# Ordering the readers of a DMA transpose later, and a batch's front earlier, in a planned attention and mixer kernel

## The chip, the cores and the metric

The kernel runs on one core of a Trainium2 chip. Its metric is the device time of one execution in microseconds. It was 430.25 us in the median of six runs before the change (424.12 to 431.26). The core has five engines that each work through their own instructions in order: TensorE (PE) multiplies matrices into eight PSUM banks, VectorE (DVE) and ScalarE (ACT) do elementwise work and read those banks, GpSimd (POOL) and SyncE (SP) here mostly issue DMAs. Engines wait for one another, and for DMAs, by semaphores. A wait at the head of an engine's queue holds all that stands behind it.

## The reference

Eight batches go through attention with a low-rank projection and then through a mixer. With B = 8, H = 8 heads, S = 1024, D = 64, 64 projected keys, and H*D = 512 columns:

```python
k_proj = einsum('ks,bhsd->bhkd', E, k)
v_proj = einsum('ks,bhsd->bhkd', F, v)
scores = q @ k_proj^T / sqrt(64)
x = softmax(scores) @ v_proj                     # to (batch, 1024, 512)
h = (relu(x^T @ w_tok1) @ w_tok2)^T              # mixes tokens: 1024 -> 256 -> 1024
u = x + h
out = u + relu(u @ w_ch1) @ w_ch2                # mixes channels: 512 -> 1536 -> 512
```

Inputs and output are float32; the kernel multiplies in bfloat16.

## The kernel before, in words

**Two halves of a batch's work.** The *front* of a batch is all up to u: the projection of k and v (`kv_proj`, L467 and L470), scores and exponential (`scores`, L580 and L589), attention's product with v and its division into x_sb (`attend`, L603, L615, L620), the first token product (`token1`, or from batch 2 on `token1_seven`, L761, in seven products for eight), and the second token product with the addition of x that writes u (`token2`, L654 and L665). What follows is the channel mixer, in two blocks of 512 rows for a batch, so 16 blocks j. For each block there are four sums of quarters of turned u (`s_sums`, L694, on VectorE), six sets of up-products (`up_set`, L937), and the down-products (`down_block`, L1038), again with seven products in place of eight: three up-products of a set read turned u itself, four read the sums S. Results are added to u into one of three tiles o and stored (L1067).

**Turned u.** The up-products need u with channels on partitions. From batch 1 on, `token2` lets SP issue a DMA transpose (L674) after each four of its eight row blocks: the first half of a batch goes to uT0, the second to uT1. Each of these tiles exists once, so a transpose also has to wait until the last product of the batch before has read its half. The returned job is kept in `turned_u[b, i]`. From batch 2 on, q and the projected k are turned by DMA transposes on SP's queue too (L545 into qT, L499 from kb into kT).

**Loads take turns with transposes.** `tie` adds a dependency. k and v of batch b are loaded in four pieces by GpSimd; the first three go behind the first transpose of batch b-2 (`load_kv`), the second transpose of batch b-2 goes behind the third piece, the fourth piece behind that transpose, and the two q loads behind it as well (`q_transpose`). GpSimd's queue, L329 and L1067, holds these loads and the stores of o in one order.

**The planner.** All work is first given to a `Planner` as jobs: an engine, a time that it occupies the engine (`occ`), a time until its result is there (`lat`), what it reads and writes, and a due time (`prio`). `plan()` then walks through a model of the five engines, and at each step starts the job that can start first, among nearly equal ones the most urgent. Sorted by planned start, the jobs are emitted; `pin()` fixes the resulting order on each engine. The model's times are nowhere in the built program: only its order is, and on the chip each instruction starts when its engine and its semaphores let it. In the model a u transpose occupies the DMA for 3.5 us and ends after 5.5 us (`sp` adds 2.0), and a job on another engine that depends on it starts 1.0 us after that at the earliest. A transpose has no due time of its own; it takes one from the jobs behind it.

**Due times of a front.** `front(b, begin, end)` lists the units of a front with a cost each and spreads their due times evenly from begin to end. The main loop adds the channel mixer of batch b, and then the front of batch b+1 with begin = at - 62 and end = at - 14, where `at = 2 * TU * (b + 1)` is the model's time for the batch and TU is 24.65. So front and mixer of neighbouring batches interleave on TensorE. The front of a batch also adds `load_kv` for the batch after it.

Of the kernel before, what the change touches and what calls it, by code (L numbers as in the profile page):

```python
# [183 lines left out]
def kernel(  # L184
# [59 lines left out]
    def bank(b):  # L244

        return banks[b.at]
# [59 lines left out]
    def pe(n, cols, fn, **kw):  # L306
        t = n * MM[cols]
        return pl.add("PE", t, t, fn, **kw)

    def dve(cols, fn, ps=True, **kw):  # L310
        t = cols / 960 + 0.07 if ps else cols / 1920 + 0.07
        return pl.add("DVE", t, t + 0.09, fn, **kw)
# [5 lines left out]
    def sp(t, fn, **kw):  # L318
        return pl.add("DMA", t, t + 2.0, fn, **kw)
# [88 lines left out]
    for n, (src, dst) in enumerate(((EF[1], FT_sb), (EF[0], ET_sb))):  # L408
        b = Bank("S", full=False)
# [44 lines left out]
    def kv_proj(b, h0, hn, due, block=False):  # L454
        hs = slice(h0, h0 + hn)
        hk = slice(h0 % (H // 2), h0 % (H // 2) + hn)
        heads = range(h0, h0 + hn)
        bk = Bank(stream[0], full=False)

        def view():  # L460
            return bank(bk).rearrange("p (h d) -> p h d", d=D)

        def mm(lo, hi):
            t = view()
            for si in range(lo, hi):
                a, z = si == 0, si == NSI - 1
                nc.tensor.matmul(  # L467
                    t[0:KP, 0:hn], ET_sb[:, si, :], k_sb[:, hs, si, :], start=a, stop=z
                )
                nc.tensor.matmul(  # L470
                    t[KP : 2 * KP, 0:hn], FT_sb[:, si, :], v_sb[:, hs, si, :], start=a, stop=z
                )

        cols = hn * D
        reads = ["ET", "FT"] + [(n, h) for n in "kv" for h in heads]
        pl.add(
            "PE", 8 * max(cols, 128) / 2400 + 0.22, 8 * max(cols, 128) / 2400 + 0.22,
            lambda: mm(0, NSI), reads=reads, takes=[bk], prio=due,
            after=[("vb", i, h) for i in range(2) for h in heads],
        )  # L480
        src = [lambda: view()[0:KP, 0:hn], lambda: view()[KP : 2 * KP, 0:hn]]
        if block:
            k_to = [kb[i * KP : (i + 1) * KP, hs, i, :] for i in range(2)]
        else:
            k_to = [kp[:, hk, i, :] for i in range(2)]
        v_to = [vb[i * KP : (i + 1) * KP, hs, i, 0:D] for i in range(2)]

        def copy(to, n):
            return lambda: nc.scalar.copy(out=to, in_=src[n]())

        for i in range(2):
            act(cols, copy(k_to[i], 0), writes=[("kb" if block else "kp", i, h if block else h % (H // 2)) for h in heads], uses=[bk])
        for i in (1, 0):
            act(cols, copy(v_to[i], 1), writes=[("vb", i, h) for h in heads], uses=[bk])

    def k_transpose_dma():
        sp(
            2.5,
            lambda: nc.sync.dma_start_transpose(  # L499
                out=kT.rearrange("p h c k -> p h (c k)"), in_=kb.rearrange("p h r d -> p (h r d)")  # L500
            ),
            reads=[("kb", i, h) for i in range(2) for h in range(H)],
            writes=[("kT", i, h) for i in range(2) for h in range(H)], prio=None,
        )

    def k_transpose(h0, hn, due):
        hs = slice(h0, h0 + hn)
        heads = range(h0, h0 + hn)
        bk = Bank(stream[0], full=False)

        def view():
            return bank(bk).rearrange("p (h k) -> p h k", k=KP)

        def mm():
            for h in range(hn):
                nc.tensor.matmul(
                    view()[:, h, :], kp[:, h0 % (H // 2) + h].rearrange("k r d -> k (r d)"),
                    ident[:KP, :KP], start=True, stop=True,
                )

        pe(
            hn, 64, mm, reads=[("kp", i, h % (H // 2)) for i in range(2) for h in heads], takes=[bk],
            prio=due,
            after=[("kT", i, h) for i in range(2) for h in heads],
        )
        act(
            hn * KP, lambda: nc.scalar.copy(out=kT[0:D, hs, 0, :], in_=view()[0:D, 0:hn]),
            writes=[("kT", 0, h) for h in heads], uses=[bk],
        )
        act(  # L530
            hn * KP,
            lambda: nc.scalar.copy(out=kT[D : 2 * D, hs, 1, :], in_=view()[D : 2 * D, 0:hn]),
            writes=[("kT", 1, h) for h in heads], uses=[bk],
        )
# [114 lines left out]
    def token2(b, si, due):  # L649
        bk = Bank(stream[0], full=False)  # L650

        def mm():
            for t in range(TC):
                nc.tensor.matmul(  # L654
                    bank(bk), wt2_sb[:, t, si::NSI], hT_sb[:, t, :],
                    start=(t == 0), stop=(t == TC - 1),
                )

        pe(
            TC, 512, mm, reads=["wt2"] + [("hT", t, hp) for t in range(TC) for hp in range(HP)],  # L660
            takes=[bk], prio=due,
        )
        dve(
            512,
            lambda: nc.vector.tensor_add(  # L665
                out=u_t[b % 2][:, si, :], in0=bank(bk), in1=x_sb[:, si, :]
            ),
            reads=[("x", h, si // NJ) for h in range(H)], writes=[("u", b % 2, si)], uses=[bk],
        )
        if si % NJ == NJ - 1:  # L670
            i = si // NJ
            j = sp(
                3.5,
                lambda: nc.sync.dma_start_transpose(  # L674
                    out=uT_t[i].rearrange("p s dc q -> p (s dc) q"),
                    in_=u_t[b % 2][:, i * NJ : (i + 1) * NJ].rearrange("p s d -> p (s d)"),
                ),
                reads=[("u", b % 2, n) for n in range(i * NJ, (i + 1) * NJ)],
                writes=[("uT", i, n) for n in range(HP)], prio=None,
            )  # L680
            turned_u[b, i] = j

    def quarter(j, sh, dh):
# [481 lines left out]
    def load_kv(b):  # L1165
        first, second = turned_u.get((b - 2, 0)), turned_u.get((b - 2, 1))
        jobs = load_group(b, "kv", first)
        if second:
            tie(second, jobs[2])
            tie(jobs[3], second)  # L1170
            rest[b] = jobs[3:]

    def front(b, begin, end):
        units = []

        def unit(cost, f):
            units.append((cost, f))

        hn = H // 2 if b == 1 else H
        for i in range(H // hn):  # L1180
            if b == 1:
                unit(1.9 * hn / H, lambda t, i=i: kv_proj(b, i * hn, hn, t))
                unit(0.9 * hn / H, lambda t, i=i: k_transpose(i * hn, hn, t))
            else:
                unit(1.9, lambda t: kv_proj(b, 0, H, t - EARLY, True))
                unit(0.0, lambda t: k_transpose_dma())
            if b == 1:
                for hp in range(2 * i, 2 * i + 2):
                    unit(0.4, lambda t, hp=hp: q_transpose_pe(hp, t))
        if b + 1 < B:  # L1190
            unit(0.0, lambda t: load_kv(b + 1))
        unit(0.4, lambda t: scores(0, t))
        unit(0.4, lambda t: scores(1, t))
        for h in range(H):
            if h + 2 < H:
                unit(0.4, lambda t, h=h: scores(h + 2, t))
            for half in range(2):
                unit(0.25, lambda t, h=h, half=half: attend(h, half, t))
        if b < 2:
            for n in range(TC):  # L1200
                unit(1.8, lambda t, n=n: token1(n, t))
        else:
            unit(3.2, lambda t: token1_seven(b, t))
        for si in range(NSI):
            unit(0.55, lambda t, si=si: token2(b, si, t))
        total = sum(c for c, _ in units)
        done = 0.0
        for c, f in units:
            f(begin + (end - begin) * done / total)
            done += c  # L1210
# [4 lines left out]
    for b in range(B):  # L1215
        for j in (2 * b, 2 * b + 1):
            s_sums(j)
            for m in range(SETS):
                up_set(j, m)
            down_block(j)  # L1220
        if b == 1:
            tok1_sums()
        if b + 1 < B:
            at = 2 * TU * (b + 1)
            if b > 0:
                q_transpose(b + 1)
            front(b + 1, at - 62, at - 14)
    gate = mybir.DependencyInfo(mybir.DependencyClass.Sync, mybir.DependencyReason.DATA)
    plan = pl.plan()
    name_of = {}  # L1230
# [51 lines left out]
```

## Time and profile before

The profiled execution took 431.77 us; its span, first to last instruction, is 429.8 us.

| what | value |
| --- | --- |
| median of six runs (range) | 430.25 us (424.12 to 431.26) |
| profiled execution: time, span | 431.77 us, 429.8 us |
| mean granted TensorE clock | 0.989 |
| busy: PE, DVE, ACT, POOL | 415.4, 342.2, 228.9, 66.3 us |
| up-products (L937), four groups | 58.2, 57.6, 55.9 and 28.8 us |
| down-products (L1038), two groups | 104.1 and 78.4 us |
| u transposes, issue to landing (min, median, max) | 4.2, 5.0, 10.9 us (14 of them) |
| stores of o, issue to landing, median | 3.8 us |
| loads of k, v, q from batch 1 on, median | 7.5, 9.6, 9.9 us |

Busy times are shares of the span in which an engine has an instruction running. In the table of groups a row has the source line, engine, operation, operands and shapes, the count, the busy time, the mean length of one, and the idle time of the engine before such instructions with its releaser. The list of waits gives for each pair of waiter and releaser the time in total, how often, and the longest. A wait for several things is put down to the one that came last. PEclk is the granted TensorE clock as a share of full speed.

### The profile page before, as it was taken

Reading aid. Unit: us, or ns where it says so; the run is one execution under the profiler, and the core shown is the slowest. Engines: PE = TensorE matmul, PEld = TensorE weight load, DVE = VectorE, ACT = ScalarE, POOL = GpSimd, SP = SyncE. Lnnn points to the kernel's source line nnn. Section 1 sums busy time; section 2 is a strip of 40 time slices with the busy share of each in tenths; the row PEclk is TensorE's granted clock in tenths of the full one; section 3 lists DMA queues with packets and bytes.
Section 4 is the critical chain, followed back from the end, with each engine's and each line's share of the span. In section 5 each row is a group of like instructions: output and inputs, shape, how many; then the busy total and the mean of one; then the engine's idle time right before and its main releaser. Section 6 shows DMA issues by size and latency. Waiting matters only on the chain.

```text
span 429.8 us, 9371 instructions
## 1 busy us (share of the span) xinstructions
PE 415.4 (97%) x3755; PEld 345.0 (80%) x3778; DVE 342.2 (80%) x837; ACT 228.9 (53%) x434; POOL 66.3 (15%) x104
## 2 busy tenths in 40 slices
PE   9899999999999999969999999999999999999995
PEld 4587886788788878858878897888878898888884
DVE  2469978789798987957878996889868998968674
ACT  2858885266546454634455645375555644354430
POOL 8443221022021212110111200212100000000000
PEclk9999999999999999997999999999999999999998
DMA  9999999977999895979739895699850502250222
GB/s 164 207 200 206 206 207 177 229 119 186 186 153 229 141 221 104 198 87 147 195 76 196 170 143 156 91 217 165 170 121 6 143 1 103 46 148 15 84 99 99
DMA packets 96651, 62.47 MB, mean 145 GB/s; under 512 B 62048, under 2 KB 92256, under 8 KB 96608
## 3 DMA queue, kind: packets, MB, share of 16 engines
q0 software_dynamic: 34944, 45.09, 52.7%
q1 hardware_dynamic: 61584, 16.52, 22.5%
q8 instruction: 29, 0.48, 0.4%
q10 hardware_dynamic: 80, 0.26, 0.2%
q14 instruction: 14, 0.11, 0.1%
HBM read 59.24 MB, written 16.78 MB: 177 GB/s over the span
## 4 chain that ended last, share of the span: by engine, by line
PE 83%; DMA 7%; DVE 7%; issue 1%; ACT 1%; POOL 1%; POOLq 0%; DVEq 0%
PE ps L1038 33%; PE ps L937 31%; PE ps L654 5%; PE ps L761 3%; PE ps L603 3%; DMA q_sb<-in_q_dram 3%; PE ps L467 3%; DMA uT<-u 3%; PE ps L580 2%; DMA v_sb<-in_v_dram 2%; DVE x_sb L620 1%; DVE u L864 1%; PE ps L634 1%; DVE S L694 1%; DVE G L972 1%
## 5 line engine op out<-in xcount | busy, mean ns | idle before, releaser
L1038 PEld LDWEIGHTS <-G 128*128 128x128 bf16 x1344 | 130.4, 98 | 20.4 <-issue 0.7
L1038 PE MATMUL ps<-wc_sb,G 128*128 128x256 bf16 x768 | 104.1, 274 | 0.2
L959 ACT ACTIVATE G<-ps 128x512 bf16<-128x512 f32 x96 | 57.1, 597 | 67.6 <-PE ps L937 66.7
L937 PEld LDWEIGHTS <-wc_sb 128*128 128x128 bf16 x768 | 74.3, 98 | 12.9 <-issue 0.3
L1038 PE MATMUL ps<-wT,G 128*128 128x256 bf16 x576 | 78.4, 274 | 0.1
L937 PEld LDWEIGHTS <-wT 128*128 128x128 bf16 x576 | 55.7, 98 | 10.5 <-issue 1.3
L937 PE MATMUL ps<-uT,wc_sb 128*128 128x256 bf16 x384 | 58.2, 274 | 0.2
L937 PE MATMUL ps<-S,wc_sb 128*128 128x256 bf16 x384 | 57.6, 273 | 0.1
L937 PE MATMUL ps<-S,wT 128*128 128x256 bf16 x384 | 55.9, 276 | 0.5 <-DVE S L694 0.4
L620 DVE TENSOR_TENSOR x_sb<-ps,rdn 128x256 bf16<-128x256 f32 x128 | 49.9, 415 | 0.8
L1067 POOL DMA_DIRECT2D out_dram<-o x30 | 16.3, 545 | 211.1 <-DVE o L1073 145.4
L589 ACT ACTIVATE a<-ps 128x512 bf16<-128x512 f32 x64 | 37.7, 600 | 19.2 <-PE ps L580 16.5
L665 DVE TENSOR_TENSOR u<-ps,x_sb 128x512 bf16<-128x512 f32 x56 | 37.3, 686 | 11.6 <-PE ps L654 6.8
L965 ACT COPY ua<-ps 128x512 f32<-128x512 f32 x48 | 28.2, 587 | 29.9 <-PE ps L937 29.5
L918 DVE CUSTOM_DVE_ANT_0 G<-ps,ua 128x512 bf16<-128x512 f32 x48 | 32.8, 684 | 10.3 <-ACT ua L965 10.2
L918 DVE CUSTOM_DVE_ANT_0 g<-ps,ub 128x512 bf16<-128x512 f32 x48 | 32.8, 685 | 10.2 <-PE ps L937 10.0
L972 DVE TENSOR_TENSOR G<-G 128x512 bf16<-128x512 bf16 x96 | 38.8, 418 | 1.7
L615 DVE RECIPROCAL rdn<-ps 128x4 f32<-128x4 f32 x128 | 21.2, 177 | 21.4 <-PE ps L603 19.1
L603 PE MATMUL ps<-vb,a 128*128 128x130 bf16 x256 | 31.5, 222 | 3.9 <-DVE x_sb L620 3.9
L965 ACT COPY ub<-ps 128x512 f32<-128x512 f32 x48 | 28.0, 584 | 12.8 <-PE ps L937 12.2
L978 ACT COPY ps<-ps 128x512 f32<-128x512 f32 x48 | 27.9, 581 | 8.3 <-PE ps L937 2.8
L654 PE MATMUL ps<-hT_sb,wt_sb 128*128 128x512 bf16 x99 | 29.1, 379 | 0.5 <-issue 0.2
(90 smaller groups left out, 524.5 us busy)
## 6 DMA issues: line engine op xcount, KB each, us to landing
out_dram<-o POOLq DMA_DIRECT2D x30, 512.0 KB, 3.8
k_sb<-in_k_dram POOLq DMA_DIRECT2D x14, 512.0 KB, 7.5
v_sb<-in_v_dram POOLq DMA_DIRECT2D x14, 512.0 KB, 9.6
q_sb<-in_q_dram POOLq DMA_DIRECT2D x14, 512.0 KB, 9.9
wc_sb<-in_moe_w_ch_dram POOLq DMA_DIRECT2D x6, 256.0 KB, 12.1
wc_sb<-in_moe_w_ch_dram POOLq DMA_DIRECT2D x4, 384.0 KB, 12.4
k_sb<-in_k_dram POOLq DMA_DIRECT2D x4, 256.0 KB, 7.3
v_sb<-in_v_dram POOLq DMA_DIRECT2D x4, 256.0 KB, 7.8
```

The lines of the kernel that those rows point to most:

```text
L589: lambda: nc.scalar.activation(out=a_t[h % 4], in_=bank(bk), func=ACT.Exp, scale=scale),
L603: nc.tensor.matmul(view()[:, 2 * jj : 2 * jj + 2].rearrange("p c d -> p (c d)"), a_t[h % 4][:, j * P : (j + 1) * P], vb[:, h].rearrange("k ...
L620: lambda: nc.vector.tensor_tensor(out=x_sb[:, 4 * half : 4 * half + 4, h * D : (h + 1) * D], in0=view()[:, :, 0:D], in1=rdn[:, :, None].to ...
L654: nc.tensor.matmul(bank(bk), wt2_sb[:, t, si::NSI], hT_sb[:, t, :], start=(t == 0), stop=(t == TC - 1),)
L665: lambda: nc.vector.tensor_add(out=u_t[b % 2][:, si, :], in0=bank(bk), in1=x_sb[:, si, :]),
L918: nc.vector._custom_dve(TENSOR_ADD_SAT, out=out, in0=in0, in1=in1, s0=FMAX, s1=0.0)
L937: nc.tensor.matmul(t[:, c, :], w1_of(n, dd, 2 * m + c), a_of(j, n, dd), start=(n in (1, 7) and c == 0 and dd == 0), stop=(c == 1 and dd == 1),
L959: lambda: nc.scalar.activation(out=G[:, n, cs], in_=view(src), func=ACT.Relu),
L965: 512, lambda: nc.scalar.copy(out=dst, in_=view("y")), writes=[(name, s % 2)],
L972: 512, lambda: f(out=G[:, n, cs], in0=in0, in1=in1), ps=False, reads=deps,
L978: 512, lambda: nc.scalar.copy(out=view("y"), in_=view("x")), takes=[bk["y"]],
L1038: nc.tensor.matmul(view(where[n])[:, t, :], G[:, G_OF[n], cc, t * P : (t + 1) * P], w2_of(n, cc), start=(n in opens and t == 0 and cc == 0 ...
```

## The change

Two places change. After a u transpose of batch 2 or later has been added, its `lat` is raised by 3.0, so that the model has its result after 8.5 us in place of 5.5. And the front of batch b+1, from batch 3 on (b > 1), gets due times that are 4 us earlier at both ends.

```diff
@@ token2
                 writes=[("uT", i, n) for n in range(HP)], prio=None,
             )
+
+            if b > 1:
+                j.lat += 3.0
             turned_u[b, i] = j
@@ main loop
             at = 2 * TU * (b + 1)
             if b > 0:
                 q_transpose(b + 1)
-            front(b + 1, at - 62, at - 14)
+            ahead = 4 if b > 1 else 0
+            front(b + 1, at - 62 - ahead, at - 14 - ahead)
```

The built program has the same instructions on every engine, in another order on TensorE, VectorE, ScalarE and SP; GpSimd's order is the same.

## The prediction

> **What bounds the kernel now.** I read the page's busy table and its 40 slices first: which engine is full, and where is it not?
>
> ```profile
> span 429.8 us, 9371 instructions
> ...
> PE 415.4 (97%) x3755; PEld 345.0 (80%) x3778; DVE 342.2 (80%) x837; ACT 228.9 (53%) x434; POOL 66.3 (15%) x104
> ...
> PE   9899999999999999969999999999999999999995
> ...
> PEclk9999999999999999997999999999999999999998
> ```
>
> TensorE bounds it. Apart from start and end there is one hole, the 18th slice with a 6, and the next slice has the only lowered clock. So nothing short of removing matmuls can shorten the rest, and this change removes none. The list of waits names the hole:
>
> ```profile
> POOL v_sb L329 <- DMA uT<-u: 32.9, 5, 10.5
> ...
> DVE S L694 <- DMA uT<-u: 4.5, 2, 4.1
> ...
> PE ps L603 <- DVE x_sb L620: 3.9, 1, 3.9
> ```
>
> TensorE waited once, 3.9 us, for an x_sb multiplication; VectorE stood 4.1 us on a transpose of u at a sum S (L694). The timeline there (start, length, what, in brackets the idle time before it and its releaser) and then the chain (start, length) show that these are one event:
>
> ```profile
> 180.35 3.78 SPq L674 DMA_TRANSPOSE uT<-u  x1
> ...
> 180.79 0.55 POOL L1067 DMA_DIRECT2D out_dram<-o  x1 [1.51 <-DVE o L1103]
> ...
> 191.30 0.43 DVE L694 TENSOR_TENSOR S<-uT 128x512 bf16<-128x512 bf16 x1 [4.12 <-DMA uT<-u]
> 191.64 0.42 DVE L620 TENSOR_TENSOR x_sb<-ps,rdn 128x256 bf16<-128x256 f32 x1
> 191.84 0.75 POOL L329 DMA_DIRECT2D v_sb<-in_v_dram  x1 [10.50 <-DMA uT<-u]
> ...
> 192.11 0.59 PE L603 MATMUL ps<-vb,a 128*128 128x130 bf16 x4 [3.92 <-DVE x_sb L620]
> ```
>
> ```profile
> 180.35 10.92 DMA uT<-u
> 191.28 0.02 issue
> 191.30 0.43 DVE S L694
> 191.72 0.34 DVE x_sb L620
> ```
>
> The second transpose of batch 3 (counted from 0) needs 10.92 us to land. A store of o issued 0.44 us after it lands after 10.0 us; the median store takes 3.8, the median transpose 5.0. The two slow each other. No matmul wants that S yet; but VectorE's queue is in order, the sum stands ahead of an x_sb multiplication, and attention's next product (L603) needs the PSUM bank that this frees. The bill closes: 10.92 + 0.02 + 0.43 + 0.34 + 0.04 to the next matmul = 11.75 us after the issue; the matmuls between the issue and that L603 fill 7.85 us (58 of 256 columns at 109 ns, 4 of 512 at 216, 12 of 130 at 55, paces from the chain: six in 0.66, four in 0.86, two in 0.11). 11.75 - 7.85 = 3.90, measured 3.92.
>
> The stall costs more than itself. Busy time by stage:
>
> ```profile
> core 0: us, PE busy (x) PEld busy (x) DVE busy (x) ACT busy (x) POOL busy (x), PEclk, DMA share, GB/s
> 182.70:193.40 10.70, 6.78 (x61) 5.56 (x59) 5.60 (x19) 3.89 (x8) 1.55 (x3) 0.90 0.71 87
> 193.40:204.20 10.80, 10.80 (x84) 8.72 (x83) 8.20 (x25) 4.54 (x8) 0.70 (x1) 0.78 0.92 147
> ```
>
> Lost clock is 0.10 x 10.7 + 0.22 x 10.8 = 3.45 us of TensorE work. Cut finer, PEclk is 1.00 from 188 to 191.3 us and 0.51 from there to 198.2: it falls at the end of the stall.
>
> **The change, part by part.** No instruction is added or removed on any engine; the planner's costs and due times alone change, so everything is a matter of order. I read the order in which the built program's instructions stand, before and after. Through batch 1's transposes nothing moves.
>
> *3 us more latency of the transpose.* The S sums fall back in VectorE's queue. For the stalled half, 23 VectorE instructions stood between the last add that the transpose reads and its first sum; now 46 do, the rest of attention among them. The transpose itself still cannot start before the last product that reads the old uT1. From that product to the first matmul that depends on the sum, through VectorE's queue or directly, I count the matmuls by shape and price them as above. Stalled half (batch 3): 132 + 3 + 24 = 14.39 + 0.65 + 1.32 = 16.4 us, where 7.85 were. Second halves of batches 2, 4, 5, 6, 7: 20.9, 14.7, 17.4, 12.8, 12.2 us (before 16.7, 8.5, 9.1, 9.1, 10.9). First halves of 2 to 7, counted from the token product behind which they start: 14.7, 15.1, 14.5, 14.5, 13.0, 13.3 (before 14.2, 11.6, 9.6, 10.7, 10.7, 9.6). What is needed is a landing plus about 0.8 us. Landings in the trace are 5.4, 10.9, 4.3, 5.5, 4.8, 6.4 for the second halves and 4.2 to 6.5 for the first, which also need about 1.2 us from product to issue. Even a collision as bad as the worst in every half (11.75) fits under the smallest cover, 12.2. So the stall goes: -3.92 us, and the clock stays up.
>
> What the clock gives back is where a rule and the row part. The row says 3.45 us. The Trainium skill, "TensorE: Matmul & The Clock Gate", section "Part 1: The HAM clock gate", has the array at half rate until about 3.4 us of sustained work, an estimate of 3.4 / 2 = 1.7 us per cooling. By the rule the sum is 3.92 + 1.7 = 5.6 us, by the row 3.92 + 3.45 = 7.37. I take the row, since it is of this very stall. The page's threshold, about 3.4 us of idle time, agrees with it: this stall just reached it. It speaks against expecting the whole gain in every execution: a shorter stall may have cost no clock.
>
> *Fronts 4 us ahead.* Attention of a front ends 2.6 to 4.8 us of matmuls earlier against the products around it, the first token product starts 3 to 5.5 us earlier, and the projection of k and v for the front after it comes earlier too. That last one is the dangerous side: it needs the second half of v, which the GpSimd queue holds behind the second transpose (10.50 in the timeline), with the q loads behind it. Cover from that transpose's possible issue to the next projection was 26.4, 25.5, 25.0, 25.8 us behind batches 2 to 5; it is 22.7, 20.5, 20.5, 21.8. Needed in the worst case seen: 10.92 + 0.57 to the issue + 5.36 landing of v = 16.9. It lies beside other work, 3.6 us to spare, cost nothing; without that cover it would cost its excess and the clock. GpSimd's own order is unchanged, so its stores are not passed by anything.
>
> SP's queue does change, around the u transposes of batches 3 and 4. Batch 4's kb transpose goes ahead of q's, and the second half of its q behind the first u transpose; batch 5's kb stands between the halves of q. kT needs 6.7 us from the projection's last matmul (159.39) to landing (166.06) and has 15.7 us or more. The late half of q has about 19 us after the token product; a u and a q transpose in a row took 8.1 us (117.95 to 126.03). Batch 5's kb waits for q to land: at worst 10.92 + 12.2 (191.28 to 203.47) = 23.1 us after the u transpose's issue, while kb itself is ready after 20.5 + 3.3 = 23.8. Cost nothing.
>
> *Bank and engine hand-overs.* Attention meets other up-products than before, and the trace of before cannot show the new meetings. Bounds: below zero is excluded on TensorE, since its gaps after 60 us other than the stall sum to under 0.6 us; above, the nearest rows are single waits of 0.4 us (PE on S, on kT), and a dozen would be 4.8 us. I take 0: VectorE was at 10.66 us of 10.8 in a stage (247 to 258 us) where TensorE had no gap, so full queues alone do not stop it.
>
> Sum on the profiled execution, whose own time is 431.77 us (span 429.8): 431.77 - 3.92 - 3.45 = **424.4 us**. It lies 1.5 us above the median of the six times shown, 430.25, which run from 424.12 to 431.26. The lowest is just what the sum gives without the stall, and 427.76 what one with the idle time but little lost clock would give. Against the median the forecast is -1.4%. A measurement of this kernel can tell about 2% from no change, so this counts as within it.
>
> **Rivals.**
>
> 1. *A rest of the stall stays.* Both stores and the second transpose still become ready within about 1 us of each other in the new order, in several batches, so collisions will happen. If one is longer than 10.92 us, batches 6 and 7 (12.8 and 12.2 us of cover) give way first: a 3.9 us stall gives 428.3, with the clock 431.8. For it: collisions are unchanged in kind. Against: their landings were 4.8 and 6.4, and no loads compete there.
>
> 2. *Slower: the earlier projections outrun v.* From a transpose landing about 3.6 us later than the worst one, the projection of the next front waits for v with its cover shortened by 4 to 5 us, in each batch that collides. At 3.9 + 3.45 us a time, two such waits give 439.1, over 2% up. For it: waits of 10.5 us behind this transpose in the GpSimd queue. Against: one landing in twelve exceeded 6.5 us, and two batches would each have to exceed about 14.5.
>
> 3. *Small waits.* A dozen hand-overs of 0.4 us: 424.4 + 4.8 = 429.2, no difference from before. For it: fuller VectorE stages. Against: above.
>
> 4. *The change does nothing*, because the sums stand where they stood. The built order excludes it.
>
> 5. *Over 2% faster* would need under 421.6, 2.8 us more than the stall returns; only a faster start could give it, and the start is untouched.
>
> **How the numbers follow.** Stall gone, 0.74, 424.4 with 422.8 to 426 around it; a rest or small waits, 0.16, 427 to 432; slower by over 2%, 0.08; faster by over 2%, 0.02. The range takes the first case and the nearer part of the second: 422.8 to 429. Chances: faster 0.02, same 0.90, slower 0.08.
>
> **What would show it.** Right: no slice of TensorE under 9 between start and end, no lowered clock before the end, the waits of S on uT and of L603 on x_sb gone or under 0.5 us, while landings of 8 to 11 us may still be there, covered, and GpSimd's v loads still wait for uT. Wrong: TensorE idle at L467 or L470 for v_sb (rival 2), S idle in batches 6 or 7 (rival 1), or many short waits on banks (rival 3). The prediction rests most on collisions being no worse than the one seen.

## The result, and the profile after

The changed kernel takes **423.85 us** in the median of 29 runs (423.32 to 424.98), the kernel before 429.81 us in the median of 64 (424.09 to 431.99). The measured ratio is 0.9901 with a 95% interval of 0.988 to 0.9922; it leaves out the slower executions of before, so it is nearer to 1 than that of the medians (423.85 / 429.81 = 0.986). It is faster, by less than the 2% from which a measurement of this kernel counts. Forecast were 424.4 us and -1.4%.

The profiled execution took 423.97 us. Its page, the rows for TensorE and its clock:

```profile
span 422.0 us, 9362 instructions
...
PE 411.1 (97%) x3760; PEld 342.7 (81%) x3778; DVE 341.2 (81%) x837; ACT 227.0 (54%) x434; POOL 66.3 (16%) x104
...
PE   7899999999999999999999999999999999999996
...
PEclk8999999999999999999999999999999999999999
```

The hole in the 18th slice is gone, and with it the lowered clock; what clock is lost before the last matmul is lost in the first 11.2 us. In the list of waits of the kernel after, the two rows that made the chain, S on uT and L603 on x_sb, no longer appear. GpSimd still waits for transposes:

```profile
POOL v_sb L329 <- DMA uT<-u: 30.5, 5, 8.3
```

The timeline at the place of the old stall (lines are three or more further down than before):

```profile
180.96 2.31 SPq L674 DMA_TRANSPOSE uT<-u  x1
181.73 0.55 POOL L1070 DMA_DIRECT2D out_dram<-o  x1 [1.86 <-DVE o L1106]
...
188.34 0.75 POOL L329 DMA_DIRECT2D v_sb<-in_v_dram  x1 [6.05 <-DMA uT<-u]
...
192.23 0.75 DVE L620 TENSOR_TENSOR x_sb<-ps,rdn 128x256 bf16<-128x256 f32 x2
195.29 0.42 DVE L697 TENSOR_TENSOR S<-uT 128x512 bf16<-128x512 bf16 x1
```

The transpose is issued 0.6 us later than in the profile of before and meets the store again, this time 0.77 us behind it; it lands after 6.8 us, at 187.8. VectorE now does all of attention first and comes to the sum at 195.3, with 7.5 us in hand. Busy time in three stages of 10 us there:

```profile
177.00:187.00 10.00, 10.00 (x97) 8.66 (x96) 9.42 (x30) 5.48 (x10) 1.10 (x2) 1.00 0.81 196
187.00:197.00 10.00, 10.00 (x100) 9.03 (x98) 9.12 (x26) 5.01 (x10) 2.26 (x3) 1.00 0.83 128
197.00:207.00 10.00, 10.00 (x91) 7.83 (x89) 8.17 (x19) 6.68 (x14) 0.55 (x1) 1.00 0.82 151
```

TensorE, the first busy column, fills every one of them at a clock of 1.00.

In this profile the milder meeting with the store alone would have removed the stall: 6.8 us and the 0.8 us behind a landing make 7.6, within the old cover of 7.85 us. (Cover is the matmul time between a transpose's issue and the first matmul that depends on its sum.) So the profile after does not by itself show what the longer cover is worth; the experiments have to. Batch 4 does need it here: its second transpose, with a store 0.34 us behind, lands after 8.6 us, more than the 8.5 us of cover that its sum had before.

The two traces can be balanced. From the first up-product to the start of the last matmul before takes 392.14 us (32.31 to 424.45), after takes 384.84 (32.75 to 417.59): 7.30 us less. The stall of 3.92 and 3.41 us of lowered clock (half rate for 6.83 us in the trace's record of the clock) make 7.33. The rest of the spans' difference of 7.73 lies outside: the first up-product comes 0.44 us later, and the span ends 0.87 us sooner after the last matmul.

### The profile page after: what moved, and what is told of

It reads as the page before. It is cut to its first block, busy times and chain, and to the rows that moved or that the text cites. A ratio compares the mean times of both kernels' runs of the same rounds, so it can differ in the third digit from the quotient of the medians.

```text
span 422.0 us, 9362 instructions
## 1 busy us (share of the span) xinstructions
PE 411.1 (97%) x3760; PEld 342.7 (81%) x3778; DVE 341.2 (81%) x837; ACT 227.0 (54%) x434; POOL 66.3 (16%) x104
## 4 chain that ended last, share of the span: by engine, by line
PE 87%; DVE 6%; DMA 4%; issue 1%; POOL 1%; POOLq 0%; DVEq 0%
PE ps L1041 34%; PE ps L940 32%; PE ps L654 6%; PE ps L764 4%; PE ps L467 3%; PE ps L603 3%; DMA q_sb<-in_q_dram 3%; PE ps L580 3%; DMA v_sb<-in_v_dram 2%; DVE u L867 1%; DVE x_sb L620 1%; PE ps L634 1%; DVE S L697 1%; PE ps L564 1%; DVE u L746 1%
## 5 line engine op out<-in xcount | busy, mean ns | idle before, releaser
L940 PE MATMUL ps<-S,wT 128*128 128x256 bf16 x384 | 54.7, 273 | 0.4 <-DVE S L697 0.4
L665 DVE TENSOR_TENSOR u<-ps,x_sb 128x512 bf16<-128x512 f32 x56 | 36.3, 685 | 9.9 <-PE ps L654 6.6
L603 PE MATMUL ps<-vb,a 128*128 128x130 bf16 x256 | 31.4, 220 | 0.0
L940 PE MATMUL ps<-uT,wT 128*128 128x256 bf16 x192 | 28.8, 273 | 0.2
## 6 DMA issues: line engine op xcount, KB each, us to landing
wc_sb<-in_moe_w_ch_dram POOLq DMA_DIRECT2D x6, 256.0 KB, 12.3
```

The source lines that it names most:

```text
L603: nc.tensor.matmul(view()[:, 2 * jj : 2 * jj + 2].rearrange("p c d -> p (c d)"), a_t[h % 4][:, j * P : (j + 1) * P], vb[:, h].rearrange("k ...
L665: lambda: nc.vector.tensor_add(out=u_t[b % 2][:, si, :], in0=bank(bk), in1=x_sb[:, si, :]),
L940: nc.tensor.matmul(t[:, c, :], w1_of(n, dd, 2 * m + c), a_of(j, n, dd), start=(n in (1, 7) and c == 0 and dd == 0), stop=(c == 1 and dd == 1),
```

## The experiments

The theory: VectorE's queue held a sum nearer to a transpose than a slow transpose takes to land; the latency term moves it, and the time comes from nothing else in the change. A transpose is slow when a store of o meets it. Rivals: the gain is the earlier fronts'; or the transpose is slow at that place by itself; or, after what the profile shows, the new order only spaces store and transpose better.

**Latency alone.**

```diff
-            ahead = 4 if b > 1 else 0
+            ahead = 0
```

> Only the 3 us of latency, fronts due as before. Theory (cover: the sum S must not stand in VectorE's queue nearer to the transpose than it takes to land): covers of the second halves of batches 2 to 7 are 21.1, 17.0, 20.6, 17.3, 11.7, 13.5 us, the stalled one 17.0 where 7.8 were and 11.75 are needed; stall gone, 423.5 to 424.5 us. Rival (the gain is the fronts', which bring attention away from the transpose): stall stays, 428 to 431.

Measured: 424.08 us (424.0 to 424.27, 4 runs), ratio to before 0.9849 (0.9817 to 0.9882). The latency term gives the whole difference. The fronts are not needed for it. In its profile the store comes at the same moment as the transpose, which lands after 5.7 us, so this run does not separate the cover from the milder meeting either; the run with one transpose does.

**Fronts alone.**

```diff
-            if b > 1:
-                j.lat += 3.0
```

> Only the fronts 4 us ahead, latency as before. Theory (cover): second halves 16.6, 8.6, 8.3, 8.3, 9.2, 10.9 us; with a collision as in the profile of before (11.75 needed) batch 3 still stalls 3.1 us, and batches 4 and 5 may if their stores now collide; 427 to 432 in most executions. Rival (fronts): 423.5 to 424.5.

Measured: 428.87 us (428.39 to 431.69, 10 runs), ratio 0.9972 (0.9952 to 0.9992). In its profile (428.83 us) TensorE and VectorE wait as the covers say:

```profile
PE ps L603 <- DVE x_sb L620: 3.9, 3, 1.7
```

```profile
DVE S L695 <- DMA uT<-u: 7.0, 3, 2.5
```

One stall has become three, at 190.4, 240.8 and 291.5 us, of 0.6, 1.6 and 1.7 us: batches 3, 4 and 5, whose covers are 8.6, 8.3 and 8.3. The one in batch 4:

```profile
230.88 1.99 SPq L674 DMA_TRANSPOSE uT<-u  x1
...
231.22 0.55 POOL L1068 DMA_DIRECT2D out_dram<-o  x1 [2.36 <-DVE o L1104]
...
239.45 0.43 DVE L695 TENSOR_TENSOR S<-uT 128x512 bf16<-128x512 bf16 x1 [2.45 <-DMA uT<-u]
...
240.79 0.27 PE L603 MATMUL ps<-vb,a 128*128 128x130 bf16 x2 [1.63 <-DVE x_sb L620]
```

The transposes land after 7.85, 8.55 and 8.63 us, and the waiting matmul starts 1.36 us after each landing, since more of VectorE's work than one sum and one multiplication lies between. Landing and 1.36 us, less the cover, are 0.6, 1.6 and 1.7 us: the covers give each stall.

What is new in batches 4 and 5 is less the cover, which hardly changed (8.5 and 9.1 before), than the meeting: their stores now come 0.34 us behind the transposes, in the profile of before 2.6 and 2.0 us, where the landings were 4.3 and 5.5. None of the stalls lowered the clock (PEclk 1.00 in the stages before and after the latter two). That is why this kernel is near 429 and not near 432: 384.84 us from first up-product to last matmul have become 389.51, and the stalls are 3.9 us of that.

**One transpose alone.**

```diff
-            if b > 1:
+            if (b, i) == (3, 1):
                 j.lat += 3.0
...
-            ahead = 4 if b > 1 else 0
+            ahead = 0
```

> Fronts as before, 3 us more latency for one transpose alone, the second half of batch 3. Theory (the whole difference is the one stall): its cover is 12.3 us in place of 7.8, the others 16.6, 8.6, 9.0, 9.0, 10.9 as before; 424 to 425. Rival (margin in every batch matters, the one stall was only the one in the profile): 426 to 430.

Measured: 424.46 us (423.79 to 425.29, 4 runs), ratio 0.9858 (0.9828 to 0.9887). Its profile is the cleanest proof of the cover, for the collision happened in it, with the store 0.44 us behind as before. The transpose issued at 179.81 us lands after 10.5:

```profile
179.81 3.67 SPq L674 DMA_TRANSPOSE uT<-u  x1
180.25 0.55 POOL L1070 DMA_DIRECT2D out_dram<-o  x1 [1.51 <-DVE o L1106]
...
190.35 0.76 DVE L697 TENSOR_TENSOR S<-uT 128x512 bf16<-128x512 bf16 x2 [0.68 <-DMA uT<-u]
```

VectorE even waits 0.68 us for it, and TensorE has no gap, since 12.3 us of matmuls lie over it. So a slow transpose is harmless when it is covered, and better spacing is not what removes the stall. The one stall was the whole difference: with its single job shifted the median is within 0.6 us of the full change.

**A store cut, at the wrong place.**

```diff
+            if (j, sh) == (6, 1):
+                cs = slice(0, 8)
```

> The kernel before, with one store cut to 8 of its 512 columns: the second store of batch 3's first block, issued 0.44 us after the slow transpose (the rest of its rows is left out of the output). Theory (the two slow each other): the transpose lands in 4.5 to 6.5 us, under the cover of 7.8 less 0.8 for the sum and what follows; no stall, 424 to 425. Rival (the transpose is slow by itself, or by its place behind the loads): it lands in about 11 us, 428 to 431.

Measured: 430.3 us (426.74 to 432.0, 20 runs), ratio 1.0 (0.998 to 1.0019), the rival's number. But the edit missed: the store that follows the slow transpose belongs to block 4, the block of batch 2 that is being finished then; block 6 stores some 53 us later. The expectation named the wrong block, and the run tells nothing of the theory. It is a second look at the kernel before, and a useful one. In its profile (426.74 us, the quickest of the 20 executions) the transpose lands after 9.5 us and the stall is shorter:

```profile
PE ps L603 <- DVE x_sb L620: 2.5, 1, 2.5
```

This one did not lower the clock: PEclk is 1.00 in the stages from 188 to 198 us. 2.5 us over 424.2 is all that it cost.

**The right store cut.**

```diff
-                1.5, lambda: queue.dma_start(out=out_v[b, :, rows, cs], in_=o_t[os[sh]][:, :, cs]),
+                1.5, lambda: queue.dma_start(out=out_v[b, :few, rows, cs], in_=o_t[os[sh]][:few, :, cs]),
...
+            few = 8 if (j, sh) == (4, 1) else P
```

> The kernel before, now with the store that really follows the slow transpose cut to 8 of 128 partitions (the second store of block 4, GpSimd at 180.8 us; the rest of those rows is left out of the output). Theory (store and transpose slow each other): the transpose lands in 4.2 to 5.7 us, within the cover of 7.8; no stall, 423.5 to 424.6. Rival (the transpose is slow at this place for another reason): landing 8 to 11 us, 428 to 431.

Measured: 424.23 us (423.91 to 424.32, 4 runs), ratio 0.9874 (0.982 to 0.9927).

```profile
180.23 3.01 SPq L674 DMA_TRANSPOSE uT<-u  x1
180.67 0.54 POOL L1068 DMA_DIRECT2D out_dram<-o  x1 [1.51 <-DVE o L1104]
185.95 0.76 POOL L329 DMA_DIRECT2D v_sb<-in_v_dram  x1 [4.75 <-DMA uT<-u]
186.70 1.50 POOL L329 DMA_DIRECT2D q_sb<-in_q_dram  x2
186.97 0.39 DVE L694 TENSOR_TENSOR S<-uT 128x512 bf16<-128x512 bf16 x1
```

The issues are where they were, 0.44 us apart, and the order is that of before; only 120 of the store's 128 partitions are missing. The transpose lands after 5.2 us, the sum no longer waits, and TensorE has no gap. The three other executions took no longer, while only 9 of the 64 executions of before are under 425 us. So the store's traffic is what slowed the transpose. From first up-product to last matmul this takes 384.84 us, as the change does: without the stall the orders before and after are equally long.

**How much cover there is.** The kernel after, with the second transpose of batch 3 repeated; each repetition waits for the one before it.

```diff
-                lambda: nc.sync.dma_start_transpose(
+                lambda: [nc.sync.dma_start_transpose(
...
-                ),
+                ) for _ in range(2 if (b, i) == (3, 1) else 1)],
...
-            tc.add_manual_dep(new[-1], name_of[tied[j]], gate, reason="loads and transposes take turns")
+            tc.add_manual_dep(new[0], name_of[tied[j]], gate, reason="loads and transposes take turns")
```

> The kernel after, with the second transpose of batch 3 done twice in a row, the second time behind the landing of the first. Theory (cover 16.4 us): landing 6.8 + about 5 = 12 us after the issue, 12.6 with the sum; no stall, 423.5 to 424.5. Rival (transpose traffic itself costs, covered or not): about 2 us more, 426.

Measured: 424.09 us (423.32 to 424.47, 4 runs), ratio 0.9872 (0.9827 to 0.9917). Landing 11.1 us after the first issue, no gap.

> The same transpose three times. Theory: about 17 us to landing, 17.7 with the sum, 1.3 us over the cover of 16.4; v's second half then comes at 23 against 20.8 + 1.3; in all 1 to 3 us of short waits that do not lower the clock, 425 to 427. Rival (any wait on a transpose costs the clock too): 429 to 431. Rival (traffic): 428.

Measured: 424.38 us (424.2 to 424.81, 4 runs), ratio 0.9885 (0.9833 to 0.9937). The time missed the range from below; the waits named were there, but small. The added repetitions landed after 4.25 and 4.29 us, not 5, so the last came 15.4 us after the first issue. With the sum and an addition that stands behind it in VectorE's queue, 1.1 us, that is 16.5, just over the cover of 16.4. VectorE waited 1.0 us for the landing, TensorE 0.1 at the first matmul behind it and 0.1 at another. Then v's second half, issued behind the last landing, reached SBUF at 201.69, just after its projection was due:

```profile
201.74 0.11 PEld L470 LDWEIGHTS <-FT_sb 128*64 128x64 bf16 x1 [0.27 <-DMA v_sb<-in_v_dram]
```

In all, from first up-product to last matmul, this takes 385.75 us, 0.9 more than the change and 0.6 more than with two transposes, at a clock of 1.00.

> The same transpose four times. Theory: about 22 us to landing, 22.9 with the sum, 6.5 us of stall on the sum, about 1 more on v's second half, and 3.4 us of lowered clock: 433 to 436. Rival (clock price of 1.7 us): 432 to 433. Rival (traffic): 430.

Measured: 431.21 us (429.81 to 432.04, 10 runs), ratio 1.0033 (1.0009 to 1.0058). The chain in its profile (429.81 us):

```profile
180.72 6.35 DMA uT<-u
187.07 0.02 issue
187.09 4.25 DMA uT<-u
191.34 0.02 issue
191.35 4.28 DMA uT<-u
195.63 0.02 issue
195.65 4.24 DMA uT<-u
199.90 0.02 issue
199.92 0.43 DVE S L697
200.34 0.61 DVE da L1094
```

```profile
PE ps L1041 <- DVE da L1094: 3.9, 1, 3.9
```

From issue to the waiting matmul, a down-product, are 201.00 - 180.72 = 20.28 us. Less the cover of 16.4, counted from the order before anything ran, that is 3.9; TensorE waited 3.89. The forecast of 433 to 436 was too high by the repetitions' landing, and by v: its second half landed at 205.9 and no projection waited for it. So the three runs agree with the cover: no stall 4 us below it, waits of tenths at its edge, and 3.9 us when it is exceeded by as much, with the clock on top. The added transpose that was covered cost 0.2 us in the medians, not the 2 us of the rival of traffic, which falls. The clock in the profile with four:

```profile
195.00:201.00 6.00, 2.11 (x21) 1.75 (x18) 1.23 (x4) 1.51 (x3) 0.54 (x1) 0.98 0.47 88
201.00:205.00 4.00, 4.00 (x23) 2.93 (x23) 3.75 (x9) 1.53 (x4) 1.72 (x3) 0.60 0.75 123
```

Lost are 0.02 x 6 + 0.40 x 4 = 1.7 us of TensorE work.

No version beat these: the change, latency alone, one half alone and the cut store all end at 423.8 to 424.5, where TensorE has no gap of over 0.25 us left after the first 60 us.

## Why the prediction was right

- *The stall and its chain.* Right in place, cause and size: 3.92 us, taken out by the order of VectorE's queue. The prediction put the slow landing down to the store beside it from one trace; the cut store showed it. It expected collisions to go on unchanged; in the order after, the one in batch 3 was milder (6.8 us), which was luck and would have been enough there. That the cover is enough too was shown by the run with one transpose shifted.
- *The covers counted from the built order.* Right to 0.1 us where they could be tested (16.4 against 20.28 - 3.89, and the three stalls of the fronts alone), and a 10.5 us landing under 12.3 us left no gap on TensorE. The 0.8 us that the prediction added to a landing was too little for other places: it was 1.1 with four transposes and 1.36 with the fronts alone. Even 1.4 on the worst landing of before, 12.3, would have exceeded the smallest cover, 12.2, by no more than 0.1. The worst landing of the profile after is 8.6 us, so it would have fitted everywhere. Batch 7, the smallest cover with 12.2, had a landing of 7.4.
- *The clock.* For this profile the row was the right choice: 3.45 taken from it, 3.41 in the balance. The 1.7 us that the prediction worked out from the Trainium skill, "TensorE: Matmul & The Clock Gate", section "Part 1: The HAM clock gate", was not wrong either: with four transposes the stall of 3.89 us was followed by half rate for 3.41 us, a loss of 1.7. The stall of 3.92 us was followed by half rate for 6.83 us, twice as long; no run shows why. In both, the clock fell before TensorE had work again, 3.1 us (before) and 3.7 us (four transposes) into its idle time. So the prediction's "just reached it" holds only roughly: 3.1 us is less than the page's 3.4, and the measurement decides. Stalls of 1.7 and 2.5 us lowered no clock, as the prediction argued.
- *Fronts ahead cost nothing.* True with the latency term (423.85 with, 424.08 without), not by themselves: alone they brought two new stalls. What the prediction called their dangerous side, v's second half, was not what they cost. It was real all the same: with three transposes, landing 15.4 us after the first issue, v came about 0.3 us late. The prediction had put the edge at about 14.5; the small waits ahead of the projection, 0.6 us together in TensorE's starts, had moved it back.
- *Hand-overs at zero.* Right: gaps over 60 ns after the first 60 us sum to 0.21 us after, 0.50 before beside the stall.
- *The sum.* 424.4 for the profiled execution, 423.97 measured. The 0.4 is the start and tail, +0.44 and -0.87, which the sum had left as they were.
- *Rivals.* None of 1 to 3 occurred; the 29 runs span 1.7 us. The spread of before, read as one stall of differing length, fits but is not shown: two profiles of that order have stalls of 3.9 and 2.5 us, and nine of its 64 runs lie between 424.1 and 424.6, where the kernels without a stall are, but none of these was profiled.

## What to carry to other kernels

A wait on a DMA at the head of an in-order queue stalls whoever needs what stands behind it, so ask not when its own consumer is due but what is next in that queue. The work between issue and that instruction, counted from the built order and priced from the trace, is the cover, and it has to be compared with the slowest landing seen and not the median. Moving producers earlier without moving that instruction can shorten the cover elsewhere, or bring another transfer to meet the DMA; change the two together, or only the second.

## What the runs showed of the hardware that was not expected

How much a store slows a transpose hangs on fractions of a microsecond between their issues. Over all profiles, the second transposes of batches 3 to 7 that had one full store issued within 0.8 us behind them landed like this (at 0.11 us a second store followed 1.5 us later):

```
store's issue after the transpose's   transposes   landing
0.00 us                               1            5.7 us
0.11 us                               4            7.4 to 7.5 us
0.23 us                               1            7.9 us
0.34 us                               4            8.6 us (8.55 to 8.63)
0.44 us                               3            9.5, 10.5, 10.9 us
0.56 us                               5            6.3 to 6.4 us
0.77 us                               8            5.6 to 6.8 us
```

The landing grows up to 0.44 us and is shorter beyond. Between these profiles the order and the other transfers differ too, so the spacing is not isolated; but the four at 0.34 us agree to 0.1 us across two batches and three kernels. The 0.44 us of before is the worst of them, and the new order got 0.77 us in batch 3, a spacing that nobody aimed at. The cover is what makes the kernel safe from the others.

The packets show both sides of the meeting. The transpose is 2048 packets of 256 bytes in every case:

```
kernel             store's issue after the transpose's   mean (longest) packet   transpose lands
before             0.44 us                               51 ns (762)             10.9 us
one half shifted   0.44 us                               47 ns (828)             10.5 us
after              0.77 us                               23 ns (115)              6.8 us
latency alone      0.00 us                               21 ns (75)               5.7 us
store cut          0.44 us                               28 ns (773)              5.2 us
after, batch 4     0.34 us                               28 ns (678)              8.6 us
```

The store's packets of 4096 bytes reached 1332 ns in the same stretch of before and 607 ns after. The mean packet alone does not give the landing: 28 ns goes with 5.2 us and with 8.6. Why a spacing of 0.44 us is the bad one was not tried.

The other surprise is the clock's price: stalls of 1.7 and 2.5 us cost none, two stalls of 3.9 us cost 1.7 in one profile and 3.4 in another.
